# A linear-attention and token/channel-mixing kernel: residual of batches 1 to 3 through vector engine and DMA, channel stretches of 384, and batch 0's query projections on halves of the array's rows

## The chip, the cores and the metric

The kernel runs on one NeuronCore of a Trainium2 chip. The metric is the device time in microseconds (us), as the median of several executions. One further execution was taken with the hardware profiler on; the trace rows below come from it. Its instruction stream has a span of 225.5 us, and its own device time is 227.31 us.

Engines: PE is TensorE (matrix multiply; its weight loads are listed as PEld), DVE is VectorE, ACT is ScalarE, POOL is GpSimd, SP is the engine whose queue issues all DMAs here. SBUF is the on-chip memory, PSUM the accumulator memory that PE writes; the kernel uses it as tiles of 512 floats per partition, called banks here: three `ps_a`, three `ps_h` and two `ps_o`.

## The reference

```
B, H, S, D = 4, 4, 1088, 32
phi(x)  = outer product of (S1 x) and (S2 x), 8 x 8 = 64 features
q_p, k_p = phi(q), phi(k)
kv = sum over s of k_p[s] v[s]^T;   z = sum over s of k_p[s]
attn = (q_p kv) / (q_p z + 1e-6)                 # x: [B, S, H*D] = [4, 1088, 128]
h  = relu(x^T w_tok1) w_tok2                     # tokens: 1088 -> 256 -> 1088
u  = x + h^T                                     # the residual
out = u + relu(u w_ch1) w_ch2                    # channels: 128 -> 1536 -> 128
```

The four weight matrices arrive as float64 and are turned into float32 on the chip. The products of batches 1 to 3, and all of the channel mixing, use float32r operands. There each number is split into a high and a low part, and a product is three matmuls (high x high, low x high, high x low).

## The kernel before

**Stages.** For each batch b: K*b* makes the key features and the sums kv and z; Q*b* makes the query features `qp`; A*b* is the attention and token mixing: `x` = attended and divided (`divide`, L657), `t` = x times the first token weights, relu, a transpose `hT`, and `w0` to `w2` = hT times the second token weights, for the three column chunks 384, 384 and 320 of the sequence (`CHUNKS`). The result u stands transposed, [128 channels, columns].

**The residual.** u = x + h^T needs x transposed. Before, PE does this itself: `residual` (L726) issues a PE transpose for each of nine 128x128 tiles into the PSUM bank of the chunk (L733), and `second` (L780, L785 for batch 0, L789 for the others) accumulates `w` on top of it. `evict` (L760) then makes the high and low part, `uh` on ACT (L765) and `ul` on DVE (L768).

**Stretches.** The columns of u of all batches are cut into stretches U*i* (`SPANS`, L40): U0 to U2 are the three chunks of batch 0, U3 to U9 are stretches of 512, 512, 512, 512, 512, 448 and 256 columns that run over batch borders. For each stretch and each of 12 blocks of 128 hidden channels (`channel_mix`, L805): `f` = three matmuls into a `ps_h` bank (L820), `hh` = relu on ACT (L824), `hl` = the low part on DVE (L827), `s` = three matmuls into the stretch's `ps_o` bank (L833). At the end POOL adds uh + ul (L849) and DVE adds the `ps_o` bank (L852), and SP stores the result.

**Batch 0's queries.** `queries_on_pe` (L527) multiplies 128 rows (four heads of 32) of q with a spread-out S1 or S2 in which only the rows of one pair of heads are taken up by the columns of that pair: `Q0.p` is, for each of three chunks and two pairs, one plain float32 matmul into a `ps_a` bank and one into a `ps_h` bank (L553). ACT copies the first out (and for one of the pairs both), DVE or POOL multiplies. For batches 1 to 3 the features are multiplied out through DRAM (L606, L619, L622, L632).

**Order.** A planner (`Plan.run`, L138) builds the program: it walks through the operations by modelled start times and levels, and emits each on its engine; each engine then runs its own instructions strictly in the order in which they were emitted, waiting on semaphores. `LEAD` (L63) shifts the level of single operations by hand. Where the planner expects PE to wait, it issues matmuls of an identity that nobody reads (`fill`, L283). Batch 0 uses unsplit token weights (`whole`), all else the split ones (`halves`): the weights w20, w21, w22 (first channel matrix, four blocks each) and w30, w31, w32 (second) are converted by ACT (L307, L311), DVE (L314, L318, L321), POOL (L327) and split by ACT (L408) and POOL (L411).

Of the kernel before, what the change touches and what calls it, by code (L numbers as in the profile page):

```python
# [18 lines left out]
P = 128  # L19
# [16 lines left out]

WIDE = 512


def _spans():  # L40
    spans = [((0, c0, cn),) for c0, cn in CHUNKS]
    at = S
    for n in (512, 512, 512, 512, 512, 448, 256):
        parts = []
        while n:
            b, c = divmod(at, S)
            m = min(n, S - c)
# [15 lines left out]
LEAD = {  # L63
    "A0.d2": -2500.0,
    "A0.t2": -30000.0,
    "A0.w1": 7000.0,
    "A3.u1": 17000.0,
    "K3.p": 27000.0,
    "K3.s": 3000.0,
    "Q0.p11": 1000.0,  # L70
    "Q0.p20": 500.0,
    "Q2.c0": 62500.0,
    "Q3.p": 1000.0,
    "w01.low": 3500.0,
    "w03.clamp": 46000.0,
    "w11.hi": 10000.0,
    "w21.clamp": 16000.0,
    "w21.lo": -111500.0,
}
# [7 lines left out]
MARGIN = 200.0  # L87
WINDOW = 4096 / 1.2

# [27 lines left out]
class Plan:  # L117
# [20 lines left out]
    def run(self, fill):  # L138
# [12 lines left out]

        run, warm = 1400.0, None

        def clock(s, cost, mode):
            if warm is not None and s >= warm:
                return s + cost
            begin = run if s - free["pe"] < 300 else s
            at = (math.ceil(max(begin - 150, 0) / WINDOW) + 1) * WINDOW
            if mode or s + 2 * cost <= at:
                return s + 2 * cost  # L160
            return at + cost - (at - s) / 2

        while ready:
            best = []
            for op in ready:
                t = max((a.end for a in op.after), default=0.0)
                ok = True
                for k, h in enumerate(op.takes):
                    q = self.taken.setdefault(h.pool, [])
                    n = self.bufs.get(h.pool, 1) - sum(o.pool == h.pool for o in op.takes[:k])  # L170
                    if len(q) >= n:
                        old = q[len(q) - n]
                        if any(u.end is None for u in old.users):
# [20 lines left out]
            if e == "pe":  # L194
                if s - free["pe"] > FILL:
                    fill(int((s - free["pe"] - MARGIN) / (213 if warm is not None and s > warm else 427)))
                    free["pe"] = s
                mode = op.mode
                if warm is None:
                    if s - free["pe"] >= 300:  # L200
                        run = s
                    at = (math.ceil(max(run - 150, 0) / WINDOW) + 1) * WINDOW
                    if at <= s or (not mode and at <= f):
                        warm = at
                    elif mode:
                        run = f
            for h in op.takes:
# [41 lines left out]
def attn_mixer_kernel(ctx: ExitStack, tc: tile.TileContext, qT, kT, v1, s64, wt1, wt2, wc1, wc2, out):  # L249
    nc = tc.nc  # L250
    engines = {"dve": nc.vector, "pool": nc.gpsimd, "act": nc.scalar}
    bufs = {"c": 4, "tail": 4, "a_sb": 3, "ar": 3, "den": 2, "o_sb": 2, "q_sb": 2, "u": 5, "uh": 5, "ul": 5, "rec": 2, "hid": HID, "hh": HID, "hl": HID, "rows": 2, "ps_a": 3, "ps_h": 3, "ps_o": 2}

# [273 lines left out]
    def queries_on_pe(qp_hold):  # L527
# [108 lines left out]
    def mixing(b, kvz_done, qp_done, qp_hold, boost, free):  # L636
# [114 lines left out]

        residuals.append(residual(0, [last]))
# [4 lines left out]
        residuals.append(residual(1, [tr, residuals[0]]))  # L757
        second_done = []

        def evict(k, i, s, src, dst, cn):  # L760

            def high(_):
                if ("uh", k) not in box:
                    box["uh", k], box["ul", k] = new("uh", [P, WIDE], F32R), new("ul", [P, WIDE], F32R)
                nc.scalar.copy(box["uh", k][:, dst:dst + cn], t["u", i][:, src:src + cn])  # L765

            def low(_):
                nc.vector.tensor_tensor(box["ul", k][:, dst:dst + cn], t["u", i][:, src:src + cn], f32(box["uh", k][:, dst:dst + cn]), op=ALU.subtract)  # L768

            first = k not in u_holds  # L770
            u_hold = u_holds.setdefault(k, Hold("u"))
            hi = plan.add(f"{n}.uh{i}{k}", act(cn), high, [s], [u_hold] if first else (), [u_banks[i]] + ([] if first else [u_hold]), boost, order=u_first.get(k, ()))
            u_first.setdefault(k, [hi])
            u_done.setdefault(k, []).append(plan.add(f"{n}.ul{i}{k}", dve(cn), low, [hi], (), [u_banks[i], u_hold], boost))

        for i, (c0, cn) in enumerate(CHUNKS):
            if i == 2:
                residuals.append(residual(2, [second_done[0]]))

            def second(_, i=i, c0=c0, cn=cn):  # L780
# [10 lines left out]
            s = plan.add(f"{n}.w{i}", {"pe": 6 * (cn / 2.4 + 14) if b else 4 * (cn / 1.2 + 3)}, second, [m, residuals[i]] + [(is_split if b else is_whole)[1, 2 * i + f] for f in range(2)], (), [u_banks[i], hTs_hold], boost)  # L791
            second_done.append(s)
            for k, parts in enumerate(SPANS):
                d0 = 0
                for pb, p0, pn in parts:
# [9 lines left out]
    def channel_mix(segs):  # L805

        o_holds, outs = {}, {}
        for i, e0, e1 in segs:
# [3 lines left out]
            for e in range(e0, e1):  # L812
# [31 lines left out]
            if e1 == NCH:  # L844
# [85 lines left out]
```

## Time and profile before

| What | Value |
|---|---|
| device time, median of 3 runs (lowest to highest) | 227.18 us (227.15 to 227.93) |
| device time of the profiled execution | 227.31 us |
| span of its instructions | 225.5 us |
| busy PE / DVE / ACT / POOL | 217.6 / 135.4 / 113.1 / 78.6 us |
| share of the chain that ended last: PE / DVE / DMA | 79% / 8% / 7% |
| DMA traffic | 24.84 MB, mean 110 GB/s |
| granted TensorE clock, mean | 1.00 (the 2.4 GHz level) |

How to read it: an engine's busy time is the union of its instructions' durations. PE's matmuls overlap in the pipeline, so a busy PE is not yet a PE at its pace; what one matmul costs in a steady row is the distance from its start to the next one's start, which the chain of work that ended last shows directly. The time of 1.8 us between the span and the device time lies outside the instructions.

### The profile page before, as it was taken

How to read it: one execution, taken by the hardware profiler on the slowest of the kernel's cores; microseconds unless marked ns; L12 is line 12 of the kernel's file. 1: busy time of each engine (PE TensorE's matmuls, PEld its weight loads, DVE VectorE, ACT ScalarE, POOL GpSimd, SP SyncE). 2: the span in 40 equal slices, each digit the busy share in tenths (PEclk: the TensorE clock that was granted, in tenths of full speed). 3: DMA queues.
4: the chain of work that ended last, by engine and by line, in shares of the span. 5: the costliest groups of instructions: out<-in, count | busy, mean ns of one | idle time of the engine just before them, and what ended most of it. 6: DMA issues, size and time to landing. Idle time of an engine off the chain costs nothing.

```text
span 225.5 us, 4427 instructions
## 1 busy us (share of the span) xinstructions
PE 217.6 (96%) x1735; PEld 187.6 (83%) x1735; DVE 135.4 (60%) x256; ACT 113.1 (50%) x246; POOL 78.6 (35%) x77
## 2 busy tenths in 40 slices
PE   7889999899999999999999999999999999999994
PEld 7566768699989998798888887888889888889993
DVE  1499999977758644557535445245564264464563
ACT  4598577997535344422534444344433354444351
POOL 2248368799999047000602000004705022001000
PEclk9999999999999999999999999999999999999999
DMA  6999995953006972030000001385100010010010
GB/s 186 418 405 406 401 408 177 276 166 83 0 3 140 159 191 82 31 111 4 0 14 35 0 0 47 87 198 152 58 3 0 3 47 1 0 47 2 0 41 23
DMA packets 8276, 24.84 MB, mean 110 GB/s; under 512 B 1088, under 2 KB 2240, under 8 KB 8256
## 3 DMA queue, kind: packets, MB, share of 16 engines
q1 hardware_dynamic: 8256, 24.57, 34.2%
q8 instruction: 13, 0.21, 0.4%
q14 instruction: 7, 0.06, 0.1%
HBM read 21.50 MB, written 3.06 MB: 109 GB/s over the span
## 4 chain that ended last, share of the span: by engine, by line
PE 79%; DVE 8%; DMA 7%; SPq 1%; issue 1%; POOL 1%; ACT 1%; DVEq 0%
PE ps_o L833 31%; PE ps_h L820 31%; PE ps_a L708 4%; DMA doubles<-wt 4%; PE ps_a L789 4%; PE ps_a L652 3%; DMA qp<-rows 3%; PE ps_a L474 2%; DVE c L314 2%; DVE c L321 2%; DVE ps_h L318 1%; PE ps_a L733 1%; SPq L290 1%; DVE k_p L457 1%; PE ps_a L438 1%
## 5 line engine op out<-in xcount | busy, mean ns | idle before, releaser
L827 DVE SCALAR_TENSOR_TENSOR hl<-ps_h,hh 128x512 fp32r<-128x512 f32 (+4 forms) x120 | 73.0, 611 | 61.6 <-ACT hh L824 60.7
L824 ACT ACTIVATE hh<-ps_h 128x512 fp32r<-128x512 f32 (+4 forms) x120 | 64.2, 536 | 69.2 <-PE ps_h L820 56.2
L820 PE MATMUL ps_h<-uh,halves 128*128 128x512 f32 (+4 forms) x240 | 86.2, 366 | 0.7 <-DVE hl L827 0.7
L833 PE MATMUL ps_o<-hh,halves 128*128 128x512 f32 (+4 forms) x240 | 67.4, 362 | 0.0
L820 PEld LDWEIGHTS ps_h<-uh,halves 128*128 128x128 f32 x240 | 44.9, 188 | 7.4 <-DVE hl L827 1.2
L833 PEld LDWEIGHTS ps_o<-hh,halves 128*128 128x128 f32 x240 | 42.9, 188 | 5.6
L833 PE MATMUL ps_o<-hl,halves 128*128 128x512 f32 (+4 forms) x120 | 43.4, 361 | 0.0
L820 PE MATMUL ps_h<-ul,halves 128*128 128x512 f32 (+4 forms) x120 | 43.2, 360 | 0.0
L632 POOL TENSOR_TENSOR qp<-qp,br 128x544 f32<-128x544 f32 x12 | 16.2, 1369 | 44.7 <-DMA br<-rows 44.7
L833 PEld LDWEIGHTS ps_o<-hl,halves 128*128 128x128 f32 x120 | 22.5, 188 | 3.4 <-DVE hl L827 0.5
L820 PEld LDWEIGHTS ps_h<-ul,halves 128*128 128x128 f32 x120 | 22.6, 188 | 2.5
L849 POOL TENSOR_TENSOR o_sb<-uh,ul 128x512 f32<-128x512 f32 (+4 forms) x10 | 11.3, 1131 | 36.5 <-DMA outT<-o_sb 22.7
L676 POOL TENSOR_TENSOR xl<-x,xh 128x384 fp32r<-128x384 f32 x9 | 9.0, 1016 | 24.9 <-ACT xh L672 24.9
L325 POOL TENSOR_TENSOR whole<-c,tail 128x512 int32<-128x512 int32 (+3 forms) x11 | 11.7, 1070 | 12.3 <-DVE c L321 12.3
L307 ACT ACTIVATE c<-doubles 128x512 f32<-128x512 f32 (+3 forms) x17 | 10.5, 621 | 5.3 <-POOL whole L325 4.2
L457 DVE TENSOR_TENSOR k_p<-ps_a,a_sb 128x1024 f32<-128x1024 f32 (+1 forms) x12 | 10.8, 950 | 2.4 <-ACT a_sb L448 2.4
L768 DVE TENSOR_TENSOR ul<-ps_a,uh 128x384 fp32r<-128x384 f32 (+5 forms) x17 | 6.7, 421 | 8.8 <-ACT uh L765 8.7
L765 ACT CAST uh<-ps_a 128x384 fp32r<-128x384 f32 (+5 forms) x17 | 5.9, 375 | 11.8 <-PE ps_a L789 10.7
L314 DVE TENSOR_SCALAR c<-c 128x512 f32<-128x512 f32 (+3 forms) x17 | 9.0, 554 | 4.3 <-ACT c L307 4.3
L411 POOL TENSOR_TENSOR halves<-whole,halves 128x512 fp32r<-128x512 f32 (+3 forms) x11 | 11.5, 1070 | 0.0
L311 ACT ACTIVATE tail<-doubles 128x512 int32<-128x512 uint32 (+3 forms) x17 | 10.4, 618 | 1.2 <-DMA doubles<-wt 1.2
L318 DVE TENSOR_SCALAR ps_h<-c 128x512 int32<-128x512 int32 (+3 forms) x17 | 10.2, 616 | 0.2
(71 smaller groups left out, 242.2 us busy)
## 6 DMA issues: line engine op xcount, KB each, us to landing
qp<-rows SPq DMA_DIRECT2D x6, 544.0 KB, 4.7
br<-rows SPq DMA_DIRECT2D x12, 272.0 KB
doubles<-wc SPq DMA_DIRECT2D x6, 512.0 KB, 10.0
v_sb<-v SPq DMA_DIRECT2D x4, 594.0 KB, 5.9
k_sb<-kT SPq DMA_DIRECT2D x4, 576.0 KB, 15.3
q_sb<-qT SPq DMA_DIRECT2D x4, 544.0 KB, 7.3
doubles<-wt SPq DMA_DIRECT2D x4, 512.0 KB, 7.0
doubles<-wt SPq DMA_DIRECT2D x4, 384.0 KB
```

The lines of the kernel that those rows point to most:

```text
L307: nc.scalar.activation(f32(t["c"]), f32(high), AF.Abs)
L314: nc.vector.tensor_scalar(f32(t["c"]), f32(t["c"]), LEAST, MOST, op0=ALU.max, op1=ALU.min)
L318: nc.vector.tensor_scalar(t["ps"], t["c"], 3, 0x3FFFFFFF, op0=ALU.logical_shift_left, op1=ALU.bitwise_and)
L325: engines[e].tensor_tensor(dst(), t["c"], t["tail"], op=ALU.add)
L411: engines[e].tensor_tensor(halves[w, i][:, 1], f32(whole[w, i] if w < 2 else t["c"]), f32(halves[w, i][:, 0]), op=ALU.subtract)
L457: nc.vector.tensor_tensor(t["k_p"][:pn, t0 * H:t1 * H], a.unsqueeze(3).broadcast_to([pn, n, R, R]), t["sb", t0][:pn, :n].unsqueeze(2).broa ...
L632: engines[e].tensor_tensor(qp[:, p, cs], qp[:, p, cs], t["br"][:, p, cs], op=ALU.mult)
L820: nc.tensor.matmul(h_ps[:, :cn], lhsT=part(2, at[2][e][0], l, at[2][e][1] * P, P), rhs=r[:, :cn], start=(m == 0), stop=(m == 2))
L824: nc.scalar.activation(t["hh"][:, :cn], t["h"][:, :cn], AF.Relu)
L827: nc.vector.scalar_tensor_tensor(t["hl"][:, :cn], t["h"][:, :cn], 0.0, f32(t["hh"][:, :cn]), op0=ALU.max, op1=ALU.subtract)
L833: nc.tensor.matmul(outs[i][:, :cn], lhsT=part(3, at[3][e][0], l, at[3][e][1] * P, P), rhs=r[:, :cn], start=(e == 0 and m == 0), stop=(e == ...
L849: engines[e].tensor_tensor(outs["sb", i][:, :cn], f32(box["uh", i][:, :cn]), f32(box["ul", i][:, :cn]), op=ALU.add)
```

## The change

Three things change, and the order with them.

1. **Residual.** For batches 1 to 3, x is turned in blocks of 32x32 by DVE (`xb`), written to DRAM by one DMA (`xm`), and read back by four DMAs (`xT`, 32 partitions each) so that the blocks land transposed. `second` starts its bank itself, and DVE adds bank and `xT` into a new SBUF tile `us` (`put`). `uh` is taken from `us` by ACT, `ul` by DVE or POOL, and the last addition reads `us` instead of a rebuilt uh + ul. Batch 0 keeps the PE transposes.
2. **Stretches.** U3 to U11 are eight stretches of 384 and one of 192 columns.
3. **Batch 0's queries.** Both head pairs are projected by one operation: each matmul takes only the 64 rows of its pair, so that the two of a kind lie on different halves of the array's rows and write to different banks. All four banks are taken at once.

The table `LEAD` has other entries, the planner's model of PE's clock is a single instant, and its cost for a triple of matmuls is 3 x cn x 0.453.

```diff
-    for n in (512, 512, 512, 512, 512, 448, 256):
+    for n in (384,) * 8 + (192,):
...
+    "K1.c0": -243800.0,
+    "Q0.p0": 102700.0,
...
+            def project(_, g=g, cs=cs, cn=cn):
+
+                for kind, name in enumerate(("ps_a", "ps_h")):
+                    for p in range(2):
+                        t[kind, g, p] = bank(name)
+                    for p in range(2):
+                        rows = slice(64 * p, 64 * p + 64)
+                        nc.tensor.matmul(
+                            t[kind, g, p][:, :cn], lhsT=t["s"][rows, kind, 2 * p:2 * p + 2].rearrange("p h i j -> p (h i j)"),
+                            rhs=box["q_sb", 0][rows, cs], start=True, stop=True,
+                        )
...
-                        nc.tensor.matmul(x[:, :cn], lhsT=t["s"][:, kind, 2 * p:2 * p + 2].rearrange("p h i j -> p (h i j)"), rhs=box["q_sb", 0][:, cs], start=True, stop=True)
...
+            def turn(_):
+                t["xb"] = new("xb", [P, H, NT, D])
+                nc.vector.transpose(t["xb"].rearrange("p h t k -> p (h t k)"), t["x"].rearrange("p t h d -> p h t d"))
...
+                t["xm"] = dram.tile([P, H, NT * 32], F32, name="xm")
+                nc.sync.dma_start(t["xm"], t["xb"].rearrange("p h t k -> p h (t k)"))
...
+                    nc.sync.dma_start(t["xT"][h * D:(h + 1) * D], t["xm"][:, h].rearrange("(q d) c -> d q c", d=D))
...
-                        nc.tensor.matmul(u_ps[:, :cn], lhsT=t[l][:, f, :], rhs=part(1, 2 * i + f, r, 0, cn), start=False, stop=(k == 6), skip_group_check=True)
+                        nc.tensor.matmul(u_ps[:, :cn], lhsT=t[l][:, f, :], rhs=part(1, 2 * i + f, r, 0, cn), start=(k == 1), stop=(k == 6))
...
+                            nc.vector.tensor_tensor(
+                                box["us", b][:, a:z].rearrange("p (t q k) -> p t q k", q=parts, k=32),
+                                t["u", i][:, a - c0:z - c0].rearrange("p (t q k) -> p t q k", q=parts, k=32), xT, op=ALU.add,
+                            )
...
+                s = plan.add(f"{n}.us{i}", dve(cn), put, [s] + moved, [] if i else [us_hold], [u_banks[i], xT_hold] + ([us_hold] if i else []), boost, order=puts[-1:])
...
+                        nc.vector.tensor_tensor(outs["sb", i][:, d0:d0 + m], box["us", b][:, c0:c0 + m], outs[i][:, d0:d0 + m], op=ALU.add)
```

**Where the order moves.** The first place is DVE ahead of the first `ul` of U0 (last row of both lists). `doubles_88` to `doubles_92` are the raw weights w11, w20, w30, w12 and w13; `k_p` at this place are the key products of batch 1. Before:

```order
L314 TENSOR_SCALAR c<-c 128x384
L318 TENSOR_SCALAR ps_h<-c 128x384
L321 SCALAR_TENSOR_TENSOR c<-doubles_91,ps_h 128x384
L457 TENSOR_TENSOR k_p<-ps_a,a_sb 128x1024 x2
L457 TENSOR_TENSOR k_p<-ps_a,a_sb 128x256
L314 TENSOR_SCALAR c<-c 128x384
L314 TENSOR_SCALAR c<-c 128x512 x2
L318 TENSOR_SCALAR ps_h<-c 128x384
L318 TENSOR_SCALAR ps_h<-c 128x512
L321 SCALAR_TENSOR_TENSOR c<-doubles_92,ps_h 128x384
L321 SCALAR_TENSOR_TENSOR c<-doubles_90,ps_h 128x512
L768 TENSOR_TENSOR ul<-ps_a,uh 128x384
```

After the change, from the third chunk of batch 0's x (first row) on:

```order
L727 TENSOR_TENSOR x<-ps_a,rec 128x384
L363 TENSOR_SCALAR ps_h<-c 128x384
L359 TENSOR_SCALAR c<-c 128x512
L366 SCALAR_TENSOR_TENSOR c<-doubles_88,ps_h 128x384
L363 TENSOR_SCALAR ps_h<-c 128x512
L366 SCALAR_TENSOR_TENSOR c<-doubles_89,ps_h 128x512
L359 TENSOR_SCALAR c<-c 128x384
L363 TENSOR_SCALAR ps_h<-c 128x384
L366 SCALAR_TENSOR_TENSOR c<-doubles_91,ps_h 128x384
L359 TENSOR_SCALAR c<-c 128x512
L363 TENSOR_SCALAR ps_h<-c 128x512
L863 TENSOR_TENSOR ul<-ps_a,uh 128x384
```

The key products, the whole of w13, the last step of w30 and the first of w21 now stand behind the first `ul`; and w11 and w20, which stood ahead of the third chunk of x, now stand behind it.

The second place is PE from batch 0's transpose `hT` to the first matmul of U0 (`ps_h<-uh`). Before (`L474` are the key sums of batch 1, the two pairs of `L785` are w0 and w1):

```order
L742 MATMUL ps_a<-ident,h 128x128 x2
L733 MATMUL ps_a<-ident,x 128x128 x3
L785 MATMUL ps_a<-whole_409,hTl 128x384
L785 MATMUL ps_a<-whole_427,hTl 128x384
L733 MATMUL ps_a<-ident,x 128x128 x3
L474 MATMUL ps_a<-v_sb,k_p 64x66 x36
L785 MATMUL ps_a<-whole_479,hTl 128x384
L785 MATMUL ps_a<-whole_563,hTl 128x384
L820 MATMUL ps_h<-uh,halves_481 128x384
```

After (`L331` are matmuls that nobody reads, `L564` the query projection of batch 1):

```order
L803 MATMUL ps_a<-ident,h 128x128 x2
L794 MATMUL ps_a<-ident,x 128x128 x3
L885 MATMUL ps_a<-whole_415,hTl 128x384
L885 MATMUL ps_a<-whole_430,hTl 128x384
L331 MATMUL ps_o<-ident 128x128 x7
L564 MATMUL ps_a<-q_sb,s_rows 64x272 x4
L939 MATMUL ps_h<-uh,halves_460 128x384
L939 MATMUL ps_h<-ul,halves_460 128x384
```

The key projection and sums of batch 1 and w1 stand behind U0's first matmuls now; three more fillers and w1 come before its first `s`.

The third place is SP's queue around batch 1's residual. After the change (the stores are those of U0 and U1; `rows`, `qp` and `br` belong to batch 2's queries):

```order
L988 DMA outT<-o_sb 128x384 x2
L828 DMA xm<-xb 128x1152
L667 DMA rows<-abT 64x544 x2
L837 DMA xT<-xm 32x4x288 x4
L335 DMA k_sb<-kT 128x1152
L680 DMA qp<-rows 128x1x1088
L683 DMA br<-rows 64x1x1088 x2
```

The write `xm` stands behind the two stores, and the reads `xT` behind the two writes of `rows`; the next key load and the query reads stand behind all of them.

## Rows read from the trace of the kernel before

**Rows 1.** The page: busy us by engine, share of the span, instructions.

```profile
PE 217.6 (96%) x1735; PEld 187.6 (83%) x1735; DVE 135.4 (60%) x256; ACT 113.1 (50%) x246; POOL 78.6 (35%) x77
```

**Rows 2.** Windows: length, busy PE, PEld, DVE, ACT, POOL, granted clock, DMA share, GB/s.

```profile
20.00:37.20 17.20, 16.36 (x213) 12.73 (x211) 16.96 (x36) 12.00 (x28) 9.70 (x11) 1.00 0.88 344
37.20:44.40 7.20, 6.46 (x38) 4.99 (x36) 6.41 (x12) 7.15 (x18) 6.53 (x5) 1.00 0.98 294
44.40:222.40 178.00, 177.95 (x1308) 156.78 (x1308) 99.34 (x185) 80.36 (x171) 54.30 (x48) 1.00 0.21 55
```

**Rows 3.** PE, timeline of the start: start, us, operation, count.

```profile
19.57 0.81 PE L553 MATMUL ps_a<-q_sb,s_spread 128*128 128x384 f32 x2
20.21 0.81 PE L553 MATMUL ps_h<-q_sb,s_spread 128*128 128x384 f32 x2
...
27.44 1.27 PE L438 MATMUL ps_a<-s_c,k_sb 128*64 128x64 f32 x36
28.64 1.56 PE L702 MATMUL ps_a<-whole,x 128*128 128x256 f32 x6
...
33.82 2.32 PE L474 MATMUL ps_a<-v_sb,k_p 128*64 128x66 f32 x72
36.07 1.56 PE L785 MATMUL ps_a<-whole,hTl 128*128 128x384 f32 x4
37.17 0.63 PE L820 MATMUL ps_h<-uh,halves 128*128 128x384 f32 x1
```

**Rows 4.** DVE, timeline of the same stretch.

```profile
26.88 0.56 DVE L666 TENSOR_TENSOR x<-ps_a,rec 128x384 f32<-128x384 f32 x1
...
29.40 2.68 DVE L457 TENSOR_TENSOR k_p<-ps_a,a_sb 128x1024 f32<-128x1024 f32 x3
32.00 1.02 DVE L314 TENSOR_SCALAR c<-c 128x384 f32<-128x384 f32 x3
32.94 1.14 DVE L318 TENSOR_SCALAR ps_h<-c 128x384 int32<-128x384 int32 x2
33.99 1.14 DVE L321 SCALAR_TENSOR_TENSOR c<-doubles,ps_h 128x384 int32<-128x384 int32 x2
35.05 0.55 DVE L768 TENSOR_TENSOR ul<-ps_a,uh 128x384 fp32r<-128x384 f32 x1
```

**Rows 5.** The chain that ended last, single pieces: start, us, engine and line, matmuls.

```profile
57.29 0.52 PE ps_h L820 x3
...
65.64 2.26 PE ps_a L652 x72
...
77.94 0.66 PE ps_a L733 x6
...
85.98 0.70 PE ps_h L820 x3
...
204.48 0.61 PE ps_o L833 x3
...
214.02 0.70 PE ps_h L820 x6
...
221.03 1.33 PE ps_o L833 x9
```

**Rows 6.** Groups by form: busy us, mean ns of one, idle before them.

```profile
L827 DVE SCALAR_TENSOR_TENSOR hl<-ps_h,hh 128x384 fp32r<-128x384 f32 x24 | 13.2, 556 | 5.9 <-ACT hh L824 5.4
...
L457 DVE TENSOR_TENSOR k_p<-ps_a,a_sb 128x1024 f32<-128x1024 f32 x8 | 9.4, 1217 | 2.4 <-ACT a_sb L448 2.4
L676 POOL TENSOR_TENSOR xl<-x,xh 128x384 fp32r<-128x384 f32 x9 | 9.0, 1016 | 24.9 <-ACT xh L672 24.9
```

**Rows 7.** POOL, timeline: the last step of w30's conversion.

```profile
35.58 1.29 POOL L327 TENSOR_TENSOR c<-c,tail 128x512 int32<-128x512 int32 x1
```

**Rows 8.** DMA issues by line: count, KB each, median us from issue to landing.

```profile
qp<-rows SPq DMA_DIRECT2D x6, 544.0 KB, 4.7
...
rows<-abT SPq DMA_DIRECT2D x6, 136.0 KB, 2.4
```

More of the change, by code (lines that the diff above doesn't have):

```diff
@@ L63 @@
 LEAD = {
[L64 to L78, printed above, removed]
+    "A0.d1": -13100.0,
+    "A0.d2": -155400.0,
+    "A0.x0": 114100.0,
+    "A1.d1": -7000.0,
+    "A1.t0": -39200.0,
+    "A1.w0": -36000.0,
+    "A1.w2": -38800.0,
+    "A2.uh06": 196600.0,
+    "A2.ul17": 117400.0,
+    "A2.w2": -130000.0,
+    "K1.c0": -243800.0,
+    "K1.c8": -222000.0,
+    "K1.v8": 11800.0,
+    "K2.p": -18100.0,
+    "K2.s": -41700.0,
+    "K3.c8": 5000.0,
+    "K3.p": 2045200.0,
+    "K3.s": -28300.0,
+    "K3.v8": 40200.0,
+    "Q0.a00": 223800.0,
+    "Q0.a11": -2800.0,
+    "Q0.a20": 87500.0,
+    "Q0.a21": 28900.0,
+    "Q0.b11": -3700.0,
+    "Q0.b21": 3300.0,
+    "Q0.p0": 102700.0,
+    "Q0.p1": 81800.0,
+    "Q0.p2": 82500.0,
+    "Q1.m01": -44000.0,
+    "Q1.m10": -1300.0,
+    "Q1.r11": -14800.0,
+    "Q3.p": -28900.0,
+    "U1.f": 21000.0,
+    "U11.f": 600.0,
+    "U2.f": -18500.0,
+    "U3.f": 39300.0,
+    "U4.f": 37400.0,
+    "U5.f": 39000.0,
+    "U6.f": 86600.0,
+    "w00.hi": 2900.0,
+    "w01.hi": 21300.0,
+    "w01.lo": -7000.0,
+    "w02.clamp": 404900.0,
+    "w02.hi": -20700.0,
+    "w02.shift": 10000.0,
+    "w03.abs": 2700.0,
+    "w03.lo": -33100.0,
+    "w03.low": -86400.0,
+    "w03.merge": 22600.0,
+    "w04.hi": 285500.0,
+    "w04.shift": 6600.0,
+    "w10.abs": 362300.0,
+    "w10.lo": -198400.0,
+    "w11.abs": 154300.0,
+    "w11.hi": 5800.0,
+    "w11.lo": -202100.0,
+    "w11.shift": -154800.0,
+    "w12.clamp": 26600.0,
+    "w12.lo": -100400.0,
+    "w13.clamp": -2414900.0,
+    "w13.hi": 13800.0,
+    "w13.lo": -19000.0,
+    "w13.low": -6700.0,
+    "w14.low": -548800.0,
+    "w15.low": -1061000.0,
+    "w20.abs": 27400.0,
+    "w20.shift": 47000.0,
+    "w22.abs": 103800.0,
+    "w22.add": -39500.0,
+    "w30.abs": 23400.0,
+    "w30.low": -174900.0,
+    "w32.add": -5700.0,
+    "w32.low": -23800.0,
 }
@@ L87 @@
 MARGIN = 200.0
-WINDOW = 4096 / 1.2
+WARMED = 5000.0
 SWITCH = 175.0
@@ L150, in run, with clock @@
         ready = [op for op in self.ops if not op.before]
-        run, warm = 1400.0, None
-        def clock(s, cost, mode):
-            if warm is not None and s >= warm:
+        def clock(s, cost):
+            if s >= WARMED:
                 return s + cost
[L157 to L161, printed above, removed]
+            return s + 2 * cost if s + 2 * cost <= WARMED else WARMED + cost - (WARMED - s) / 2
         while ready:
@@ L182, in run @@
                         s = max(s, port)
-                    best.append((s, clock(s, cost + SWITCH * (op.mode != mode), op.mode) if e == "pe" else s + cost, e, op))
+                    best.append((s, clock(s, cost + SWITCH * (op.mode != mode)) if e == "pe" else s + cost, e, op))
             assert best, [o.name for o in ready]
@@ L195, in run @@
                 if s - free["pe"] > FILL:
-                    fill(int((s - free["pe"] - MARGIN) / (213 if warm is not None and s > warm else 427)))
+                    slow, fast = max(0.0, min(s, WARMED) - free["pe"]), max(0.0, s - MARGIN - max(free["pe"], WARMED))
+                    fill(int(slow / 427 + fast / 213))
                     free["pe"] = s
                 mode = op.mode
[L199 to L206, printed above, removed]
             for h in op.takes:
@@ L750, in low, with move, back @@
             nc.vector.tensor_tensor(t["hTl"], t["hT_ps"][:, :2 * P].rearrange("p (a c) -> p a c", c=P), f32(t["hTh"]), op=ALU.subtract)
-        residuals.append(residual(0, [last]))
+        if not b:
+            residuals.append(residual(0, [last]))
+        else:
+            xb_hold, xT_hold, us_hold = Hold("xb"), Hold("xT"), Hold("us")
+            moved = []
+            def turn(_):
+                t["xb"] = new("xb", [P, H, NT, D])
+                nc.vector.transpose(t["xb"].rearrange("p h t k -> p (h t k)"), t["x"].rearrange("p t h d -> p h t d"))
+            turned = plan.add(n + ".xb", dve(SP), turn, divided, [xb_hold], [x_hold], boost)
+            def move(_):
+                t["xm"] = dram.tile([P, H, NT * 32], F32, name="xm")
+                nc.sync.dma_start(t["xm"], t["xb"].rearrange("p h t k -> p h (t k)"))
+            xm_hold = Hold("xm")
+            op = plan.add(n + ".xm", {"sp": 620.0}, move, [turned], [xm_hold], [xb_hold], boost)
+            op.bytes, op.rate = P * SP * 4, 250.0
+            for h in range(H):
+                def back(_, h=h):
+                    if h == 0:
+                        t["xT"] = new("xT", [P, 4, NT * 32])
+                    nc.sync.dma_start(t["xT"][h * D:(h + 1) * D], t["xm"][:, h].rearrange("(q d) c -> d q c", d=D))
+                op2 = plan.add(f"{n}.xT{h}", {"sp": 620.0}, back, [op], [] if h else [xT_hold], [xm_hold] + ([xT_hold] if h else []), boost, order=moved[-1:])
+                op2.bytes, op2.rate = D * SP * 4, 100.0
+                moved.append(op2)
         m = tr = plan.add(n + ".hT", {"pe": 2 * 109.0}, transpose, [relu_done], [hT_hold], [hs_hold], boost)
@@ L756, in mixing, with columns @@
             m = plan.add(n + ".hTl", dve(256), low, [m], (), [hT_hold, hTs_hold], boost)
-        residuals.append(residual(1, [tr, residuals[0]]))
-        second_done = []
+        if not b:
+            residuals.append(residual(1, [tr, residuals[0]]))
+        second_done, puts = [], []
         def evict(k, i, s, src, dst, cn):
+            c0 = CHUNKS[i][0]
+            def columns():
+                return box["us", b][:, c0 + src:c0 + src + cn] if b else t["u", i][:, src:src + cn]
             def high(_):
@@ L799, in mixing @@
                     d0 += pn
-        return second_done, residuals
+        return second_done, residuals[2:] if not b else second_done[2:]
     chain = {"f": None, "s": None}
```

75 lines of the change are left out of this document (52 added, 23 removed).

## The prediction

> **What bounds the kernel now.** I read the page first: PE is busy 96% of the span, the other engines 60% at most [rows 1]. A busy PE can still wait, so the windows come next. From 44.4 to 222.4 us PE is busy 177.95 of 178.00 us, DVE 99 and ACT 80 [rows 2]: here nothing but PE counts. From 20 to 37.2 us DVE is the full one, 16.96 of 17.20, and DMA is at 0.88 [rows 2], while part of what PE does there is fillers. So there are two stages: a start whose length DVE's list sets, up to the first matmul of U0 at 37.17 us [rows 3], and a PE-bound rest that ends with the last matmul at 221.03 + 1.33 = 222.36 [rows 5]; the remaining 3.1 us to 225.5 are the last addition and store. The granted clock is 1.00 in all of it [rows 2], so every matmul runs at the 2.4 GHz level and one price per shape does.
>
> Hence the sum: span = start of U0 + PE's work after it, waits included + tail = 37.2 + 185.2 + 3.1 = 225.5.
>
> **Prices on PE.** The chain shows what a triple costs in a gapless row: 0.52 us for 384 columns, 0.70 for 512, 0.61 for 448, and 0.70 for six of 256, thus 0.35 [rows 5]. A PE transpose of 128 columns costs 0.66 / 6 = 0.110 us [rows 5].
>
> **Residual.** For three batches nine transposes leave PE: 27 x 0.110 = 2.95 us, all in the gapless stage, so all of it counts. What comes instead: `xb` on DVE, 1152 columns; the trace has no such operation, the nearest is the 1024-column key product at 1.22 us [rows 6], so 1.37, and 2.7 if a turn ran at half the pace. Three additions per batch cost about as a `ul` of the same width (0.55 for 384 [rows 4]). DVE, ACT and POOL have 79, 98 and 124 us free in the PE-bound stage [rows 2]; about 4 us per batch and 24 more hl/hh pairs hide there, at zero, as long as no burst is longer than the three `ps_h` banks cover. Each `hl` takes 0.56 per 1.04 us of PE [rows 6, 5].
>
> The new wait is `put` on DVE, which waits for all four `xT`, with the next `hl` queued behind it and PE behind those. Trip: xb 1.4, issue 0.6, `xm` of 576 KB about as the 544 KB read, 4.7, then four issues at 0.6 and a landing as that of 136 KB, 2.4 [rows 8]: 1.4 + 0.6 + 4.7 + 1.8 + 2.4 = 10.9 us; with `xm` as quick as the 136 KB transfers, 8.6. How long does it have? Before, batch 1's attention ends at 65.64 + 2.26 = 67.9 and U3 begins at 85.98 [rows 5], 18 us later, because U0 to U2's remaining matmuls, t and w lie between; after the change the same things lie there plus batch 2's key work. Off go about 2 us for the divisions, up to 2 for the stores of U0 and U1 ahead of `xm` on SP, and 2.2 for put, uh and a `ul` on POOL at 1.02 [rows 6]. 12 us are left for 10.9. I take no wait; the margin is one to three microseconds.
>
> **Stretches.** Twelve blocks need 24 triples. Before: 5 x 24 x 0.70 + 24 x 0.61 + 24 x 0.35 = 84.0 + 14.6 + 8.4 = 107.0 us. After: 8 x 24 x 0.52 = 99.8, and 72 matmuls of 192 columns. Bounds for these: in proportion to 384 columns 0.087 each, 6.2 in all; or no less than the 0.110 of the transposes, which load the same 128 weight columns, 7.9 in all. A narrow matmul that needs a new weight load each time is nearest to the transposes: 7.9. So 107.7, **+0.7** (-1.0 by the other bound).
>
> **Batch 0's queries.** Each of the 12 projections costs 0.64 us at 384 columns [rows 3] and 0.53 in proportion at 320: 8 x 0.64 + 4 x 0.53 = 7.2 us. If two halves of the rows work side by side it is 3.6; if not, 7.2 as before. No row shows row halves, so both ends stand. This is in the start, where PE has fillers to drop, so I count it at nothing, provided that it lies off the chain. The Trainium skill (TensorEngine Tiling (Array Packing), section Key Properties) says that different tiles can execute in parallel, and also that changing the tiling mode drains TensorE. No run here shows either; by the first it would be 3.6 us of work, and a drain would be paid at most six times.
>
> **Where U0 begins.** This is the largest term. Two chains lead there.
> - DVE's list. Ahead of U0's first `ul` (35.05) the change takes away batch 1's key products (29.40 to 32.00: 2.60), two of the three steps from 32.00 to 32.94 (0.63), the 384-column one of the two from 32.94 (0.45) and both from 33.99 (1.06) [rows 4]: 4.7 us, so 30.3.
> - The data. The third chunk of x is at 26.88 [rows 4]; ahead of it now go the last steps of w11 and the first two of w20, by the same prices 0.45 + 0.45 + 0.33 + 0.60 = 1.8. Behind it PE did batch 1's key projection, 27.44 to 28.64, before the last six matmuls of t [rows 3]: another 1.1 us gone. From there nothing changes up to w0, which ended three transposes (0.3 to 0.4 us) before the key sums of 33.82 [rows 3], thus near 33.4; behind it lay uh and ul, and on PE the key sums and w1 until 37.17 [rows 3], which go behind U0. So w0 ends at 33.4 - 2.9 = 30.5, and with uh (about 0.5) and the hand-over from PE to ACT and back U0 begins near 31.5.
>
> The later one counts: **31.5**, 5.7 us earlier. Floor 30.3; ceiling 35.6 (35.05 + 0.55, nothing gained on DVE).
>
> **What is behind it now.** The work that was pulled out of the way comes back into PE's row: key projection 1.20, key sums 2.25, w1 1.10 [rows 3], together +4.55. U0's first `s` needs w30, whose merge on DVE now follows the first `ul`: 31.5 + 0.6, POOL's addition 1.29 [rows 7], w13's 1.0 and the split 1.3 give 35.7. PE has three `f` and w1, 1.56 + 1.10, until 34.2: it waits 1.5 us. Before, PE is idle for 0.74 us of the 7.2 from 37.2 to 44.4 [rows 2], and that is a floor, since a matmul's record can run on into a wait. I count the two as even, with +2 as the upper end.
>
> **Sum.** Work and waits after U0: 185.2 - 2.95 + 0.7 + 4.55 = 187.5. Span 31.5 + 187.5 + 3.1 = 222.1, against 225.5: -3.4. On the profiled execution's own 227.31 that is 223.9; its time is 0.13 above the median of the runs, so **223.8 us**.
>
> **Rivals.**
> - *Narrow float32r matmuls are not single-pass* (the other side). The smallest float32r matmul in the trace has 256 columns [rows 5]. Plain float32 costs 0.64 for 384 columns, 0.32 for 192 [rows 3]; at that price the last stretch takes 72 x 0.32 = 23 us instead of 7.9: 223.8 + 15 = 239. It decides if the 192-column triple costs over 0.47 us (where 3.4 us of gain are gone). For it speaks only that no row rules it out; against it, that 256 to 512 columns are in strict proportion. 8%.
> - *U0 begins no earlier than DVE allowed before*, because POOL, ACT or the conversion buffers hold the list up. At 35.6 the work pulled out still returns: 35.6 + 187.5 + 3.1 = 226.2 of span, 227.9. For it: POOL shares the adds, and its last steps sit behind DVE's. 12%.
> - *The residual is late.* From a trip of about 12 us on, PE pays microsecond for microsecond, in three batches: at 14 us 2 x 3 = 6, 229.8. 9%.
> - *Row halves run one after the other.* 3.6 us more in the start, about half of it on the way to x: 223.8 + 1.8 = 225.6, at worst 227.4. 11%.
> - *Reads that turn data are very slow.* If the four reads, which put blocks into other partitions, ran at nineteen times the 2.4 us, one would take 46, U3 would wait about 40, in three batches: some 340 us. By the code each run of theirs is 288 floats in a row on both sides, so 2%. The Trainium skill (VectorE: DVE Perf Modes, section The three transpose paths) gives this factor for a plain DMA copy that transposes by strides when the innermost destination stride is large; no run here shows it, and here the 32x32 turns are DVE's.
> - The forecast itself: 58%, own range 222.0 to 225.8 (floor of U0, cheap 192 columns and half of the waits; two more waits).
>
> **Range and chances.** 0.5% of 227.18 is 1.1 us, about what a measurement can tell. Faster (below 226.0): the forecast 57, most of the row-half case 8, part of the others 2: 67%. Same (to 228.3): late U0 12, the rest 4: 16%. Slower: 17%. The range leaves out the narrow-matmul case, the slow reads and most of the late residual, and takes in the floor with its best additions and the late U0: 221.3 to 228.0.
>
> **What would show it.** Right: first matmul of U0 near 31.5; no PE transposes after U0's third; 384-column triples at 0.52 everywhere, 192-column ones at 0.33; PE gapless from about 37 us; `put` waiting for PE, not for DMA; the row-half pairs starting a few tens of ns apart. Wrong: U0 after 34; a `hl` whose idle time ends with `xT`; pairs 0.3 us apart; 192-column triples near 1 us.

## The result, and the profile after

The changed kernel takes 225.27 us (median, 225.19 to 225.48), the kernel before 227.17 beside it: ratio 0.991, 95% interval 0.9895 to 0.9929. So it is 1.9 us faster, where 3.4 were forecast; 225.27 lies inside the range. Its profiled execution took 225.48 us with a span of 223.7, 1.8 shorter than before.

The page's busy line of the changed kernel (against [rows 1]) and its windows: the start up to U0, the stretch behind it, the rest (against [rows 2]; columns as there).

```profile
PE 217.3 (97%) x1896; PEld 206.7 (92%) x1896; DVE 142.4 (64%) x285; ACT 115.8 (52%) x271; POOL 80.0 (36%) x85
```

```profile
20.00:31.55 11.55, 11.18 (x96) 8.60 (x91) 11.05 (x28) 8.57 (x17) 7.71 (x8) 1.00 1.03 406
31.55:44.40 12.85, 11.33 (x92) 9.99 (x91) 11.59 (x19) 11.41 (x28) 10.81 (x10) 1.00 0.75 169
44.40:220.60 176.20, 176.19 (x1490) 172.36 (x1488) 106.75 (x214) 82.36 (x196) 53.43 (x54) 1.00 0.29 83
```

From 44.4 us on PE is as gapless as it was. The stretch behind U0's start, the middle row, is what grew: before it was 7.20 us long, with DVE, ACT and POOL 89 to 99% full and PE idle for 0.74 us [rows 2]; now it is 12.85 us long, the three are 84 to 90% full, and PE is idle for 1.5 us.

PE's timeline of the changed kernel (against [rows 3]; L600 are batch 0's projections in row halves, L713 its attention, L885 w0 and w1, L564 batch 1's query projection, L939 `f`, L952 `s`, L483 batch 1's key projection):

```profile
15.66 0.92 PE L600 MATMUL ps_a<-q_sb,s_spread 64*128 64x384 f32 x4
16.41 0.81 PE L600 MATMUL ps_h<-q_sb,s_spread 64*128 64x384 f32 x4
...
18.84 2.33 PE L713 MATMUL ps_a<-kvz,qp 128*64 128x66 f32 x72
...
27.47 1.53 PE L885 MATMUL ps_a<-whole,hTl 128*128 128x384 f32 x4 [0.23 <-ACT hTl L807]
28.83 1.73 PE L331 MATMUL ps_o<-ident 128*128 128x128 f32 x14
30.49 1.14 PE L564 MATMUL ps_a<-q_sb,s_rows 128*64 128x272 f32 x8
31.55 0.44 PE L939 MATMUL ps_h<-uh,halves 128*128 128x384 f32 x1
...
33.89 1.45 PE L885 MATMUL ps_a<-whole,hTl 128*128 128x384 f32 x4
34.88 0.81 PE L952 MATMUL ps_o<-hh,halves 128*128 128x384 f32 x2
...
38.12 1.27 PE L483 MATMUL ps_a<-s_c,k_sb 128*64 128x64 f32 x36
40.91 0.44 PE L939 MATMUL ps_h<-uh,halves 128*128 128x384 f32 x1 [1.52 <-DVE hl L946]
```

U0 starts at 31.55, as forecast. Each float32 projection is two instructions in the trace, so `x4` is the two projections of one kind: in row halves they take 0.75 us from start to start, where one of them on full rows took 0.64 [rows 3]. The last row is what was not forecast: behind the key projection PE waits 1.52 us for one `hl`. DVE's and POOL's timelines show what stands ahead of that `hl` (L359 are clamps, L456 second halves of weights):

```profile
36.43 0.56 DVE L863 TENSOR_TENSOR ul<-ps_a,uh 128x384 fp32r<-128x384 f32 x1 [0.73 <-ACT uh L860]
37.00 2.80 DVE L359 TENSOR_SCALAR c<-c 128x512 f32<-128x512 f32 x2
39.72 0.68 DVE L363 TENSOR_SCALAR ps_h<-c 128x512 int32<-128x512 int32 x1
40.32 0.54 DVE L946 SCALAR_TENSOR_TENSOR hl<-ps_h,hh 128x384 fp32r<-128x384 f32 x1
```

```profile
36.81 1.29 POOL L456 TENSOR_TENSOR halves<-whole,halves 128x512 fp32r<-128x512 f32 x1
38.11 1.40 POOL L456 TENSOR_TENSOR halves<-c,halves 128x512 fp32r<-128x512 f32 x1
```

Two clamps of 512 columns take 2.80 us, 1.38 and 1.50 each, and both end 0.3 us after one of POOL's instructions. The next row, all clamps of the changed kernel (shortest, median and longest in ns, all widths together), shows what is usual:

```profile
L359 DVE TENSOR_SCALAR c<-c x17: 285/419/1498, 6.2 to 56.2; 128x512 f32<-128x512 f32 x10, 128x384 f32<-128x384 f32 x4, 128x320 f32<-128x320 f32 x2, 128x256 f32<-128x256 f32 x1
```

Of the ten of 512 columns six took 0.42 to 0.43 us. The other four (0.67, 0.75, 1.38, 1.50) began while POOL was inside an instruction, and all four ended 0.3 us after it; two of the six began inside one as well, but in its last 0.1 us. The kernel before has the same spread:

```profile
L314 DVE TENSOR_SCALAR c<-c x17: 347/420/1237, 6.3 to 58.8; 128x512 f32<-128x512 f32 x10, 128x384 f32<-128x384 f32 x4, 128x320 f32<-128x320 f32 x2, 128x256 f32<-128x256 f32 x1
```

Its longest began at 22.82, and one at 41.52, in the stretch behind U0's start, took 1.15, each with POOL inside an instruction. So this price could be read before the change.

Single pieces of the chain that ended last (against [rows 5]) and groups by form:

```profile
210.49 0.52 PE ps_h L939 x3
...
212.05 0.65 PE ps_h L939 x6
...
215.23 0.34 PE ps_o L952 x3
```

```profile
L823 DVE STREAM_TRANSPOSE xb<-x 128x1152 f32<-128x1152 f32 x3 | 4.1, 1369 | 0.0
L905 DVE TENSOR_TENSOR us<-ps_a,xT 128x384 f32<-128x384 f32 x6 | 3.3, 552 | 2.8 <-PE ps_a L889 2.7
```

The prices are the forecast ones: 0.52 for a triple of 384 columns, 0.34 for one of 192, 1.37 for `xb`; `put` (L905) waits for PE's matmuls, not for a transfer.

### The profile page after: what moved, and what is told of

Its sections match the earlier page's. It is cut to its first block, busy times and chain, and to the rows that moved or that the text cites. A ratio compares the mean times of both kernels' runs of the same rounds, so it can differ in the third digit from the quotient of the medians.

```text
span 223.7 us, 4910 instructions
## 1 busy us (share of the span) xinstructions
PE 217.3 (97%) x1896; PEld 206.7 (92%) x1896; DVE 142.4 (64%) x285; ACT 115.8 (52%) x271; POOL 80.0 (36%) x85
## 4 chain that ended last, share of the span: by engine, by line
PE 94%; ACT 2%; DVE 2%; issue 1%; POOL 0%; POOLq 0%
PE ps_h L939 32%; PE ps_o L952 32%; PE ps_o L331 5%; PE ps_a L769 4%; PE ps_a L713 4%; PE ps_a L889 4%; PE ps_a L519 3%; PE ps_a L763 2%; PE ps_a L483 2%; PE ps_a L564 1%; PE ps_a L885 1%; PE ps_a L600 1%; PE ps_o L519 1%; PE ps_h L600 1%; ACT halves L453 1%
## 5 line engine op out<-in xcount | busy, mean ns | idle before, releaser
L946 DVE SCALAR_TENSOR_TENSOR hl<-ps_h,hh 128x384 fp32r<-128x384 f32 (+2 forms) x144 | 75.1, 532 | 51.9 <-ACT hh L943 48.5
L943 ACT ACTIVATE hh<-ps_h 128x384 fp32r<-128x384 f32 (+2 forms) x144 | 67.9, 476 | 69.0 <-PE ps_h L939 46.6
L939 PE MATMUL ps_h<-uh,halves 128*128 128x384 f32 (+2 forms) x288 | 89.1, 332 | 1.5 <-DVE hl L946 1.5
L952 PE MATMUL ps_o<-hh,halves 128*128 128x384 f32 (+2 forms) x288 | 71.9, 332 | 0.0
L939 PEld LDWEIGHTS ps_h<-uh,halves 128*128 128x128 f32 x288 | 53.3, 188 | 2.6 <-DVE hl L946 1.7
L952 PEld LDWEIGHTS ps_o<-hh,halves 128*128 128x128 f32 x288 | 50.6, 188 | 0.5
L939 PE MATMUL ps_h<-ul,halves 128*128 128x384 f32 (+2 forms) x144 | 47.4, 329 | 0.0
L952 PE MATMUL ps_o<-hl,halves 128*128 128x384 f32 (+2 forms) x144 | 47.4, 329 | 0.0
L863 POOL TENSOR_TENSOR ul<-us,uh 128x320 fp32r<-128x320 f32 (+5 forms) x15 | 9.6, 655 | 67.7 <-ACT uh L860 53.6
L939 PEld LDWEIGHTS ps_h<-ul,halves 128*128 128x128 f32 x144 | 27.1, 188 | 0.4 <-DVE ul L863 0.3
L952 PEld LDWEIGHTS ps_o<-hl,halves 128*128 128x128 f32 x144 | 27.1, 188 | 0.0
L331 PE MATMUL ps_o<-ident 128*128 128x128 f32 x82 | 13.2, 320 | 1.4 <-POOL ident masks.py:199 1.4
L331 PEld LDWEIGHTS ps_o<-ident 128*128 128x128 f32 x82 | 12.3, 230 | 2.4 <-POOL ident masks.py:199 1.4
L359 DVE TENSOR_SCALAR c<-c 128x512 f32<-128x512 f32 (+3 forms) x17 | 10.6, 638 | 3.1 <-ACT c L352 3.1
L456 POOL TENSOR_TENSOR halves<-whole,halves 128x512 fp32r<-128x512 f32 (+3 forms) x11 | 11.7, 1078 | 0.2 <-ACT halves L453 0.2
```

The lines of the kernel that those rows point to most:

```text
L331: nc.tensor.matmul(spare_ps[:, :P], lhsT=ident, rhs=ident, start=True, stop=True)
L359: nc.vector.tensor_scalar(f32(t["c"]), f32(t["c"]), LEAST, MOST, op0=ALU.max, op1=ALU.min)
L456: engines[e].tensor_tensor(halves[w, i][:, 1], f32(whole[w, i] if w < 2 else t["c"]), f32(halves[w, i][:, 0]), op=ALU.subtract)
L939: nc.tensor.matmul(h_ps[:, :cn], lhsT=part(2, at[2][e][0], l, at[2][e][1] * P, P), rhs=r[:, :cn], start=(m == 0), stop=(m == 2))
L943: nc.scalar.activation(t["hh"][:, :cn], t["h"][:, :cn], AF.Relu)
L946: nc.vector.scalar_tensor_tensor(t["hl"][:, :cn], t["h"][:, :cn], 0.0, f32(t["hh"][:, :cn]), op0=ALU.max, op1=ALU.subtract)
```

## The experiments

Theory after the result: the work is as forecast, and the missing 1.5 us are waits behind U0, above all that for the two clamps. Rivals: narrow stretches, the residual's path, or row halves that bring nothing. All kernels but those on the stretches keep the changed kernel's order of instructions, save for the edit itself; each was timed beside the kernel before. Where a kernel was not timed beside the changed one too, the difference by the two ratios to the kernel before stands with that of the times. The changed kernel itself, once more:

> The changed kernel itself, unaltered, beside the next three kernels on one chip: 225.3 us, ratio to the kernel before 0.991.

225.46 us (225.34 to 226.09), before 227.24: 0.992 (0.9906 to 0.9937).

**Clamps in another form.**

```diff
-nc.vector.tensor_scalar(c, c, LEAST, MOST, op0=max, op1=min)
+nc.vector.scalar_tensor_tensor(c, c, LEAST, most.broadcast_to([P, n]), op0=max, op1=min)   # w31, w22
```

> The two clamps of 512 columns that stand at 37.00 and 38.30 us in the changed kernel (w31's and w22's) are done by scalar_tensor_tensor against a column that holds the upper bound, in the same place of DVE's list; no other instruction moves. Theory A (POOL's running additions hold this form of clamp, and PE waits for the hl behind it): the two take 0.67 us each instead of 1.38 and 1.50, the hl at 40.32 starts near 38.8, PE's wait of 1.5 us before 40.91 shrinks to 0.3 or less, and the time falls by 1.0 to 1.5 us, to 223.8 to 224.3. Theory B (DVE's and ACT's lists are full there whatever the form of the clamp, or DMA traffic slows DVE): the hl starts at 40 or later and the time stays within 0.3 us of 225.3.

226.66 us (225.81 to 227.92), before 227.62: 0.996 (0.9941 to 0.9982), 1.4 slower than the changed kernel (1.1 by the ratios). DVE's and POOL's timelines of this kernel:

```profile
37.64 3.31 DVE L362 SCALAR_TENSOR_TENSOR c<-c,most 128x512 f32<-128x512 f32 x2
```

```profile
37.42 1.30 POOL L461 TENSOR_TENSOR halves<-whole,halves 128x512 fp32r<-128x512 f32 x1
38.76 1.65 POOL L461 TENSOR_TENSOR halves<-c,halves 128x512 fp32r<-128x512 f32 x1
```

Theory A as I had put it fell: the new form took as long (1.62 and 1.76), each ended 0.55 us after one of POOL's instructions, and PE's wait grew to 2.0 us. What this form takes beside an idle POOL, no run shows. (0.6 us of this profile's span are an earlier matter: batch 0's first projection starts at 8.07 instead of 7.40.) What both forms share is that all their operands lie in SBUF. In the changed kernel the 39 `hl` of 384 columns that start while POOL works take 0.52 to 0.56 us, the other 81 take 0.54 to 0.56; they read PSUM.

**POOL out of the way.**

```diff
-POOL: w21.add, w00.lo, w21.lo, w31.add, ... w15.lo
+POOL: w21.add, w21.lo, w31.add, ... w15.lo, w00.lo
```

> One instruction of POOL's list, the subtraction that makes the second half of w00 (36.81 us in the changed kernel, first read near 71 us), goes behind that of w15; nothing else moves. POOL then stands idle from 36.84 until ACT has the first half of w21, near 38.0. Theory A (a DVE instruction with all operands in SBUF waits for the end of the instruction that POOL is in, whatever its form; those with an operand in PSUM don't): the two clamps at 37.00 take 0.42 us each, the hl behind them starts when ACT has its hh, near 38.5 instead of 40.32, the wait of 1.5 us on PE falls below 0.4, and the time falls by 1.0 to 1.5 us. Theory B (the clamps are late for another reason, such as the DMA traffic or their own operands): they take over 1.2 us each still and the time stays within 0.3 us.

224.57 us (224.21 to 225.69), before 227.24: 0.988 (0.9861 to 0.9904), 0.9 less than the changed kernel. Timelines of POOL, DVE and PE (its L371 are the clamps, L958 `hl`, L495 the key projection, L951 `f`):

```profile
35.80 1.30 POOL L384 TENSOR_TENSOR c<-c,tail 128x512 int32<-128x512 int32 x1
38.39 1.28 POOL L468 TENSOR_TENSOR halves<-c,halves 128x512 fp32r<-128x512 f32 x1 [1.30 <-ACT halves L465]
```

```profile
37.28 0.76 DVE L371 TENSOR_SCALAR c<-c 128x512 f32<-128x512 f32 x2
...
38.74 0.56 DVE L958 SCALAR_TENSOR_TENSOR hl<-ps_h,hh 128x384 fp32r<-128x384 f32 x1
```

```profile
38.41 1.27 PE L495 MATMUL ps_a<-s_c,k_sb 128*64 128x64 f32 x36
39.60 0.44 PE L951 MATMUL ps_h<-uh,halves 128*128 128x384 f32 x1
```

With POOL idle from 37.10 to 38.39 both clamps fit into 0.76 us, and the wait of 1.5 us is gone: A, for the clamps. For every instruction whose operands lie in SBUF, as A was worded, it isn't shown: `xb` is one too, and took 1.37 us in each batch however its start lay to POOL's instructions. In time 0.9 came back, a little under A's 1.0 to 1.5: in this profile U0 starts 0.25 us later than in the changed kernel's, and the waits from 68 to 86 us are about 0.25 longer.

**Stretches of 320 and 256 at the end.**

```diff
-    for n in (384,) * 8 + (192,):
+    for n in (384,) * 7 + (320, 256):
```

> The last two stretches of the changed kernel are 320 and 256 columns instead of 384 and 192; up to about 190 us no instruction moves. Theory A (a matmul of 192 columns costs 0.111 us because it can't be quicker than its weight load, while 320 and 256 columns are in proportion to 384): 72 matmuls of 0.173 + 0.111 become 72 of 0.147 + 0.117, -1.5 us of PE work, the last addition 0.07 us longer; 223.9 us. Theory B (192 columns cost no more than in proportion): 0, 225.3 us.

224.43 us (224.21 to 224.61), before 227.24: 0.987 (0.9853 to 0.9885), 1.0 less than the changed kernel. Single pieces of its chain, of 320 and of 256 columns:

```profile
200.01 0.44 PE ps_h L939 x3
...
215.00 0.35 PE ps_h L939 x3
```

That is 0.44 and 0.35, against 0.52 and 0.34: 24 x (0.86 - 0.79) = 1.7 us by these rounded rows. A triple of 192 costs nearly what one of 256 costs, so A's prices hold; that the weight load sets the price of 192 columns is argued, not shown. Of the 1.5 us forecast 1.0 came in time: in this profile U0 starts at 31.99, 0.4 us later than in the changed kernel's, and from there to the end it is 1.3 us shorter.

**Both.**

> The edits of the two kernels before in one: stretches of 320 and 256 at the end, and w00's subtraction behind w15's. If both hold and add up: 2.5 to 3.0 us less than the changed kernel, 222.3 to 222.8 us. If the wait comes back elsewhere (POOL has one subtraction more to do later): the 1.5 us of the stretches alone, 223.8 us.

223.09 us (222.90 to 223.65): 0.982 (0.9797 to 0.9832) of before, the best of all kernels here. It is 2.4 less than the changed kernel, just under the 2.5 to 3.0 forecast; the two gains, 1.0 and 0.9, add up. Its window behind U0, in which PE has no idle time left:

```profile
31.36:44.40 13.04, 13.04 (x101) 11.72 (x100) 10.93 (x22) 12.92 (x32) 11.08 (x10) 1.00 0.75 165
```

**Full rows again.**

```diff
-lhsT=s[rows, kind, 2p:2p+2], rhs=q_sb[rows, cs]      # two halves of 64 rows
+lhsT=s[:, kind, 2p:2p+2],    rhs=q_sb[:, cs]         # all 128 rows
```

> Batch 0's query projections run over all 128 rows one after the other again, in the same places of PE's list; nothing else moves. As the prediction counted it (PE has fillers to drop there): U0 still starts at 31.5 and the time stays within 0.3 us of 225.3. Theory A (the last projections lie on the way to the attention, which now starts at 18.84 us): each group costs 2.6 us instead of 1.4, the second group pushes the third by about 1 us and the third is 1.2 us longer, so the attention starts 1.0 to 2.2 us later, U0 near 32.5 to 33.7, and the time rises by 1.0 to 2.2 us.

228.19 us (227.86 to 229.06): 2.9 more than the changed kernel (2.6 by the ratios), more than the 1.0 to 2.2 of A, and 1.0028 (1.0015 to 1.0042) of before. PE's timeline:

```profile
17.79 1.56 PE L599 MATMUL ps_a<-q_sb,s_spread 128*128 128x384 f32 x4
19.19 1.45 PE L599 MATMUL ps_h<-q_sb,s_spread 128*128 128x384 f32 x4
...
22.17 2.04 PE L712 MATMUL ps_a<-kvz,qp 128*64 128x66 f32 x62
...
34.72 0.44 PE L938 MATMUL ps_h<-uh,halves 128*128 128x384 f32 x1
```

A group of 384 columns costs 2.8 instead of 1.5 us, the attention starts 3.3 us later and U0 3.2. So the row halves lie on the way to U0 nearly in full; without them the change would gain nothing in this order.

**Residual on PE again.**

```diff
+for j in tiles of this chunk: nc.tensor.matmul(u_ps[...], lhsT=x[:, j], rhs=ident, is_transpose=True, ...)
-nc.vector.tensor_tensor(us, u_ps, xT, op=add)
+nc.vector.tensor_copy(us, u_ps)
```

> The residual of batches 1 to 3 is added by nine transposes per batch on PE again, ahead of each chunk's six matmuls; the turns on DVE, the write xm and the reads xT are gone, and put copies the sums from PSUM. Everything else keeps its place. Theory A (all 27 transposes count, at 0.110 us in the gapless stage): +2.95 us, 228.2 (227.9 to 228.5). Theory B (the move to DVE and DMA gains less since it costs waits of its own): less than +2 us.

228.70 us (228.47 to 229.05), 1.005 (1.0036 to 1.0064) of before: 3.4 more than the changed kernel (3.1 by the ratios). Its page:

```profile
PE 220.5 (97%) x1923; PEld 209.5 (92%) x1923; DVE 139.3 (61%) x282; ACT 116.0 (51%) x271; POOL 80.0 (35%) x85
```

27 more matmuls, 3.2 us more of PE, 3.2 more of span: all of it counts, and nothing of the move is given back elsewhere.

**The residual one hop later.**

```diff
-nc.sync.dma_start(xm, xb)
+nc.sync.dma_start(first, xb); nc.sync.dma_start(xm, first)
```

> Between the write xm and the reads xT of each of the batches 1 to 3, one more copy of the 576 KB from one DRAM tensor to another, on the same queue; nothing else moves. It makes the residual 4 to 6 us later. If the margin is the 1 to 3 us of the prediction: put waits for xT in batch 1 at least, PE loses 1 to 5 us, the time is 226.3 to 230. If the margin is about 4 us or more (reads issued by 75.2 us, put at 82.2): the time stays within 0.7 us of 225.3.

225.28 us (225.12 to 225.84), 0.990 of before: no change. SP's timeline of the changed kernel, SP's and DVE's of this one:

```profile
73.24 1.77 SPq L837 DMA_DIRECT2D xT<-xm  x4
```

```profile
77.63 2.18 SPq L839 DMA_DIRECT2D xT<-xm  x4
```

```profile
82.79 0.56 DVE L907 TENSOR_TENSOR us<-ps_a,xT 128x384 f32<-128x384 f32 x1 [0.55 <-DMA xT<-xm]
```

The last read is issued 4.8 us later (79.8 instead of 75.0), and now `put` waits for it, 0.55 us, which PE doesn't feel. So the margin of batch 1 is about 4.2 us. As the last read lands at 82.8 here, it lands near 78.0 in the changed kernel: 9 us after `xb` starts there (68.94).

**Batch 1's query projection out of U0's way.**

```diff
-PE: Q1.p, U0.f, U0.f, U0.f, w1       ACT: Q1.c0, Q1.c1, U0.h, ...
+PE: U0.f, U0.f, U0.f, Q1.p, w1       ACT: U0.h, ..., Q1.c0, Q1.c1
```

> Batch 1's query projection (1.07 us of PE, directly ahead of U0's first matmul in the changed kernel) and its two copies on ACT go behind U0's third f; nothing else moves. U0's first matmul then starts when the halves of w20 are there, near 30.9 instead of 31.55. Theory A (the first s waits for w30's halves, which POOL ends at 34.9 whatever PE does, and PE has slack ahead of it): the first s stays at 34.9 and the time within 0.3 us of 225.4. Theory B (the sum of the prediction, in which the start of U0 counts in full and the waits behind it don't change): 0.6 to 0.7 us less, 224.7.

226.42 us (224.92 to 228.17), before 227.49: 0.995 (0.9929 to 0.9978), 0.7 to 1.0 more than the changed kernel by the ratios: neither theory. The profiled execution took 227.46, so its rows show more loss than the median has. PE's, POOL's, ACT's and DVE's timelines (L467 is the first half of a weight):

```profile
30.70 0.42 PE L953 MATMUL ps_h<-uh,halves 128*128 128x384 f32 x1
...
35.53 0.81 PE L966 MATMUL ps_o<-hh,halves 128*128 128x384 f32 x2
...
60.50 0.44 PE L953 MATMUL ps_h<-uh,halves 128*128 128x384 f32 x1 [1.49 <-DVE c L380]
```

```profile
51.60 1.36 POOL L707 TENSOR_TENSOR qp<-qp,br 128x544 f32<-128x544 f32 x1 [2.18 <-DMA br<-rows]
```

```profile
54.24 0.62 ACT L467 CAST halves<-c 128x512 fp32r<-128x512 f32 x1 [2.79 <-POOL c L386]
```

```profile
56.69 2.57 DVE L373 TENSOR_SCALAR c<-c 128x320 f32<-128x320 f32 x2
```

U0 does start at 30.70, yet the first `s` comes at 35.53, later than the 34.88 before: w1 stands behind the projection now. The wait of 1.5 us behind the key projection is gone here too, as POOL's second subtraction comes later and the two clamps take 0.63 and 0.41. But the query's transfers are later, POOL waits 2.18 us for them, ACT waits 2.79 for a weight that POOL then finishes later, and `hh`, `hl` and the last two clamps queue behind that: they start at 56.69 instead of 55.07 (beside POOL in both kernels, 2.57 and 2.22 us for the two), and PE waits again, at 60.5. An earlier U0 gained nothing here; what it would gain with the transfers in time stays open.

## Why the prediction was right in direction, and what it mis-sized

- **Start of U0**, 31.5 forecast, 31.55 measured: the number is right, by luck. My chain counted the row halves at nothing, and with full rows U0 starts at 34.72: two errors of about 3 us cancelled. w0 ended near 29.0, not 30.5; after it PE had fillers and 1.07 us of batch 1's query projection in front of U0, which I had left where it was in time. Without that U0 starts at 30.70.
- **Batch 0's queries**, "counted at nothing": wrong as a term, though the sum hid it, since I had taken the start from other rows. The row halves are worth 2.6 to 2.9 us; the rival priced their failure at 1.8. The twelve projections take 4.3 us, where I had 3.6 for halves that run side by side.
- **Residual**, -2.95 (27 x 0.110 is 2.97): right; 3.2 by the page, 3.1 to 3.4 in time. No wait, as forecast, with a margin of 4.2 us where I had 1 to 3; the trip took 9 us, between my 8.6 and 10.9.
- **Stretches**, +0.7: right. 0.11 us per matmul of 192 columns (0.65 / 6, 0.34 / 3), as forecast; with 320 and 256 columns instead 1.0 us of time came back.
- **Work that comes back behind U0**, +4.55: right. The three terms give +2.3. If PE's row after U0 is split into work (the price of each form, as in the prediction) and waits (start to start, less that price), the work grew by 2.0 us without the fillers and by 2.6 with them.
- **Waits behind U0**, "I count the two as even": this step failed. From U0 to the last matmul's end PE took 185.2 us before and 189.0 after, 1.5 more than the 187.5 forecast; 31.55 + 189.0 + 3.1 is the measured span. By the split the waits grew from 1.9 to 2.9 us up to 44.4 us, and from 0.4 to 0.8 from 68 to 86 us. I had looked for one wait, that for w30's halves, and put it at 1.5; from U0's start to that first `s` (31.55 to 34.88) all but some 0.8 of 3.3 us are `f` and w1. I had not asked what the clamps do while POOL works, though the kernel before shows it. The cause of the largest one is shown by moving one POOL instruction; that of the smaller ones from 68 us on was not looked for.
- **Rivals.** Narrow matmuls not single-pass: fell, the triple takes 0.34, not over 0.47. U0 late, residual late, slow reads: fell. Row halves one after the other: fell too, the two of a pair start 7 ns apart.

## What to carry to other kernels

When work is pulled ahead into a stretch in which every engine is nearly full, price the waits there anew instead of carrying the old ones over. A DVE clamp from SBUF to SBUF has a price of its own beside POOL: look at what POOL does at that moment, and move the POOL instruction that nobody needs soon. And cost an edit "at nothing" only after following it to the end of its stage: here the part priced at nothing carried the gain.

## What the runs showed of the hardware

DVE's clamps (SBUF to SBUF) took 0.42 us for 512 columns beside an idle POOL (37.28 with POOL out of the way), and 1.38 and 1.50 when they began early in one of POOL's instructions, ending 0.3 us after it. Their other form, with two inputs in SBUF, took 1.62 and 1.76 there; POOL's own second instruction stretched from 1.29 to 1.40 and 1.65. The 32x32 turns of `xb`, from SBUF to SBUF with one input, took 1.37 us each time with POOL at work, and `hl`, which reads PSUM, 0.52 to 0.56.

The Trainium skill (SBUF — State Buffer, section Who interferes with whom) states this as an exclusive lock on a port pair that DVE shares with GpSimd: a tensor_scalar in a two-port mode takes it, and an instruction with two SBUF inputs contends with a GpSimd instruction that reads SBUF, whereas one with at most one SBUF input outside these modes does not contend. The trace agrees for the clamps and for `hl`, which were seen beside a working and an idle POOL; their other form and `xb` fit, but were seen only beside a working one, and no row names the mode of an instruction.

Two float32 projections on different halves of the rows ran side by side: the two, four instructions of 384 columns, took 0.75 us, where the same two on full rows took 1.36 to 1.40. A pause between work on halves and on full rows doesn't show: the last instruction of a group and the next one start 0.41 us apart, on halves (8.48 to 8.89) as on full rows before (8.07 to 8.48).
